# Issuing 32 small loads of decay rows from GpSimd instead of SyncE, in a fused attention and MLP kernel

## The chip, the cores and the metric

The kernel runs on one core of one Trainium2 chip. The metric is the device time of one launch in microseconds. The kernel before takes 765.26 us, the median of three runs (763.09 to 766.86). The execution that was profiled took 763.16 us, of which the span of its instructions is 761.2 us.

## The reference

Four sequences of 576 tokens go through causal attention with 8 heads of width 64 and a forget-gate decay, then through a first MLP with a layer norm and a residual, then through a gated MLP whose gate mixes the tokens.

```python
scores = scale * np.matmul(q, k.transpose(0, 1, 3, 2))
cum = np.cumsum(np.log(np.clip(f, 0.0001, 1.0)), axis=-1)
decay = cum[:, :, :, None] - cum[:, :, None, :]
scores = np.where(causal, -1000000000.0, scores + decay)
attn = np.exp(scores - max); attn = attn / (sum + 1e-09)
x = matmul(attn, v)                                   # 4 x 576 x 512
x = x + np.maximum(layernorm(x) * g_ln @ w_ch1, 0.0) @ w_ch2
h = np.maximum(x @ w_in, 0.0); u, v = halves of h
out = (u * (einsum('ts,bsd->btd', w_spatial, layernorm(v)) + b_spatial)) @ w_out
```

## The kernel before, in words

The 2304 tokens are cut into eight blocks of 256 tokens and a ninth part with the last 64 tokens of each sequence. For each block attention is computed, and its result goes through the first MLP in groups (`GROUPS`, seven groups of one block and one of two). The program emits attention of the blocks ahead and the MLP of a current group interleaved, by a table of positions (`SPAN`, `BEGIN`). A list scheduler then simulates the program and writes a fixed order of instructions for each engine: every engine, and every engine's queue of DMA issues, works its list strictly in order. The order is made when the kernel is built, so a change of one instruction's engine can move others.

Four blocks (the third kind, `attention`, lines 571 to 628) cover queries 256 to 575 of each sequence. They hold 4 x 8 = 32 heads, worked in 16 pairs, which this document numbers 0 to 15; pair k holds heads 2k and 2k+1. For each head `operands` (lines 325 to 343) loads q and k (line 330, tile `qk`), splits them into two operands for the scores, `x1` and `x2`, and loads four rows of cumulated decays into partitions 64 to 67 of `x2` (line 338). These rows make the decay part of the same matmul as the scores. Three buffers for `x2` are made once and filled with zeros (lines 332 to 335) and then taken in turn: `x2z0`, `x2z1`, `x2z2`, head h using buffer h modulo 3.

The scores are made in `weights` (line 359) as pairs of matmuls, one of `x2` and one of `x1`: for query tiles 2 and 3 head by head, and for tile 4 both heads of a pair together, in two column halves. So a pair has eight matmuls that read an x2 buffer, and the last of them frees the buffers of both heads. Head 2k takes the one freed by head 2k-3, and head 2k+1 the one freed by head 2k-2. With three buffers the end of pair k therefore starts two loads: that of head 2k+3, which is the second head of the next pair, and that of head 2k+4, the first head of the pair after it.

Behind the scores VectorE finds the row minimum (line 363), ScalarE takes the exponential (line 367), and the weights are written as two halves of 16 bits into `P16` (lines 319 and 380; five buffers). For tile 4 GpSimd first zeroes a part of `P16` (line 374). SyncE then transposes `P16` by DMA into `PT` (line 382), and the product with the values (line 586) follows later. The MLP's matmuls are at lines 864 and 849. At a group's end VectorE moves the sums out of PSUM (line 896, tile `t`), and GpSimd issues four DMAs that add them to the residual in DRAM (line 900). GpSimd also sums squares for the layer norm (lines 792 and 793). SyncE issues most loads of the stage: `qk`, the values `vr` (line 610), the decay rows, and the transposes.

Of the kernel before, what the change touches and what calls it, by code (L numbers as in the profile page):

```python
# [19 lines left out]
B, H, S, D = 4, 8, 576, 64  # L20
# [59 lines left out]
def f32(ap):  # L80
    return ap.bitcast(F32)
# [7 lines left out]
class Kernel:  # L89
# [235 lines left out]
    def operands(self, bh):  # L325

        nc, at = self.nc, self.at
        W, C = QW, QW + S
        qk = at.tile([P, C], F32, tag="qk", name="qk", bufs=BUFS["qk"])
        nc.sync.dma_start(out=qk, in_=self.qk[bh // H, bh % H])  # L330
        x1 = at.tile([P, C], F32R, tag="x1", name="x1", bufs=BUFS["x1"])
        if not self.x2z:
            for i in range(BUFS["x2"]):
                self.x2z.append(at.tile([P, C], F32R, name=f"x2z{i}"))
                nc.gpsimd.memset(f32(self.x2z[i][64:]), 0.0)
        x2 = self.x2z[0]
        self.x2z.append(self.x2z.pop(0))
        nc.sync.dma_start(out=f32(x2[64:68]), in_=self.decay_d[:, bh // (2 * H) * 2 * H + bh % H * 2 + bh // H % 2])
        self.copy(0, x1, qk)
        self.copy(0, x2[:64, :W], qk[:64, :W])  # L340
        nc.vector.tensor_tensor(out=x1[64:, :W], in0=qk[64:, :W], in1=f32(x1[64:, :W]), op=ALU.subtract)
        nc.vector.tensor_tensor(out=x2[:64, W:], in0=qk[:64, W:], in1=f32(x1[:64, W:]), op=ALU.subtract)
        return [(x[:, :W], x[:, W:]) for x in (x2, x1)]
# [1190 lines left out]
```

## Time and profile before

| | |
|---|---|
| median of three runs | 765.26 us (763.09 to 766.86) |
| profiled execution | 763.16 us, span 761.2 us |
| TensorE busy | 739.7 us (97%) |
| VectorE, ScalarE busy | 590.9 us (78%), 528.8 us (69%) |
| GpSimd busy | 67.4 us (9%), 102 instructions |
| decay rows | 32 issues on SyncE, 14 KB each, from 190.2 to 430.3 us |

The busy times are sums over the whole span. The stage of the 32 heads is the part from about 190 to 456 us. Times in the rows below count from the start of the span. A timeline merges like neighbours on an engine into one row, with their count behind the x; what stands in brackets is the idle time of the engine before the row and what ended it.

### The profile page before, as it was taken

The numbers are of one execution on the slowest core, as the hardware profiler recorded it, in microseconds if no ns is written. First come the engines' busy times: TensorE is split into PE (matmuls) and PEld (weight loads), VectorE is DVE, ScalarE is ACT, GpSimd is POOL, SyncE is SP. The second block draws the span as 40 slices with busy tenths as digits, with TensorE's granted clock in tenths as the row PEclk, the third lists the DMA queues.
The fourth block names the chain that finished last, engine by engine and source line by source line (L and its number), as shares of the span: only waits on it lengthen the run. The fifth ranks groups of instructions, "written<-read, shape, count | busy, mean of one in ns | idle before, by whom it ended". The sixth has DMA issues, their size and how long they took to land.

```text
span 761.2 us, 16265 instructions
## 1 busy us (share of the span) xinstructions
PE 739.7 (97%) x5912; PEld 567.9 (75%) x5912; DVE 590.9 (78%) x1569; ACT 528.8 (69%) x1320; POOL 67.4 (9%) x102
## 2 busy tenths in 40 slices
PE   8899998999999999999999999999999999999998
PEld 6788887888888877877888888644447678768686
DVE  7899799577599989989869845689456796785854
ACT  6898699576588989879857844587346764664633
POOL 6001100013102010110110100200012000000000
PEclk9999999999999999999999999999999999999999
DMA  8978694466589998988965944831025240100101
GB/s 263 295 269 274 206 266 84 89 171 105 176 167 206 198 220 183 195 189 177 201 144 116 148 84 149 213 132 56 1 22 111 70 125 1 44 21 7 57 2 62
DMA packets 164100, 104.68 MB, mean 138 GB/s; under 512 B 106147, under 2 KB 151299, under 8 KB 164021
## 3 DMA queue, kind: packets, MB, share of 16 engines
q1 hardware_dynamic: 153032, 93.06, 50.3%
q0 software_dynamic: 5376, 5.54, 5.2%
q10 hardware_dynamic: 5612, 5.06, 2.2%
q8 instruction: 46, 0.75, 0.4%
q14 instruction: 34, 0.27, 0.1%
HBM read 64.37 MB, written 15.11 MB: 104 GB/s over the span
## 4 chain that ended last, share of the span: by engine, by line
PE 63%; DVE 11%; ACT 10%; DMA 10%; issue 4%; SPq 2%; DVEq 0%; ACTq 0%
PE ph L864 16%; PE acc L849 12%; PE pb L808 8%; PE pb L809 8%; PE pb L810 8%; DMA raw<-in_moe_w_ch_dram 3%; PE s L359 3%; PE s L849 3%; DMA vr<-in_v_dram 2%; PE av L586 2%; ACT wt L744 2%; ACT P L319 2%; DMA x_d<-xT 2%; DVE P L380 1%; DMA qk<-decay 1%
## 5 line engine op out<-in xcount | busy, mean ns | idle before, releaser
L849 PE MATMUL acc<-hh,wt 128*128 128x256 f16 (+2 forms) x960 | 196.8, 295 | 3.2 <-ACT hh L875 3.2
L864 PE MATMUL ph<-xh,wt 128*128 128x256 f16 (+1 forms) x896 | 185.0, 288 | 2.0 <-DVE hl L879 2.0
L864 PEld LDWEIGHTS <-wt 128*128 128x128 f16 x1344 | 126.9, 98 | 47.4 <-issue 10.2
L849 PEld LDWEIGHTS <-wt 128*128 128x128 f16 x1344 | 128.7, 98 | 44.3 <-issue 5.3
L864 PE MATMUL ph<-xl,wt 128*128 128x256 f16 (+1 forms) x448 | 129.0, 288 | 0.0
L849 PE MATMUL acc<-hl,wt 128*128 128x256 f16 (+1 forms) x416 | 115.8, 281 | 1.1 <-DVE hl L879 1.1
L875 ACT ACTIVATE hh<-ph 128x256 f16<-128x256 f32 (+2 forms) x128 | 50.9, 397 | 45.8 <-PE ph L864 45.5
L879 DVE SCALAR_TENSOR_TENSOR hl<-ph,hh 128x256 f16<-128x256 f32 (+1 forms) x112 | 50.5, 453 | 35.9 <-ACT hh L875 35.7
L319 ACT ACTIVATE P<-sd,st 128x512 f16<-128x512 f32 (+2 forms) x128 | 70.6, 585 | 9.8 <-DVE st L370 6.9
L380 DVE SCALAR_TENSOR_TENSOR P<-sd,st,P 128x384 f16<-128x384 f32 (+2 forms) x96 | 59.2, 634 | 10.5 <-ACT P L319 10.3
L367 ACT ACTIVATE sd<-sd,st 128x384 f32<-128x384 f32 (+2 forms) x80 | 54.6, 682 | 14.4 <-DVE st L363 14.2
L359 PE MATMUL s<-x2z 128*128 128x384 f32 (+3 forms) x128 | 47.8, 382 | 1.9 <-DMA x2z<-decay_d 1.7
L363 DVE CUSTOM_DVE_ANT_0 sd<-s,mask 128x384 f32<-128x384 f32 (+2 forms) x80 | 46.0, 579 | 3.7 <-PE s L359 2.7
L900 POOL DMA_DIRECT2D x_d<-t x36 | 31.9, 1024 | 182.7 <-DVE t L896 153.1
L359 PE MATMUL s<-x 128*128 128x384 f32 (+3 forms) x128 | 41.4, 333 | 0.0
L809 PE MATMUL pb<-wsl,vh 128*128 128x288 f16 x128 | 36.6, 286 | 0.0
L808 PE MATMUL pb<-wsh,vl 128*128 128x288 f16 x128 | 36.6, 286 | 0.0
L810 PE MATMUL pb<-wsh,vh 128*128 128x288 f16 x128 | 36.4, 286 | 0.0
L810 PE MATMUL pb<-gh,woh 128*128 128x288 f16 x128 | 35.0, 286 | 0.0
L809 PE MATMUL pb<-gl,woh 128*128 128x288 f16 x128 | 35.0, 286 | 0.0
L808 PE MATMUL pb<-gh,wol 128*128 128x288 f16 x128 | 33.3, 286 | 0.0
L922 ACT ACTIVATE gh<-u 128x288 f16<-128x288 f32 x32 | 14.0, 437 | 26.5 <-DVE u L1261 26.5
(341 smaller groups left out, 1692.5 us busy)
## 6 DMA issues: line engine op xcount, KB each, us to landing
raw<-in_moe_w_ch_dram SPq DMA_DIRECT2D x32, 512.0 KB
qk<-in_qk_dram SPq DMA_DIRECT2D x32, 448.0 KB
vraw<-in_v_dram SPq DMA_DIRECT2D x5, 1024.0 KB
vr<-in_v_dram SPq DMA_DIRECT2D x16, 320.0 KB
x_d<-t POOLq DMA_DIRECT2D x36, 128.0 KB, 4.3
out_dram<-o SPq DMA_DIRECT2D x32, 144.0 KB
raw<-in_moe_w_in_dram SPq DMA_DIRECT2D x8, 512.0 KB
qk<-in_qk_dram SPq DMA_DIRECT2D x16, 192.0 KB
```

What stands on the lines that cost most here:

```text
L319: self.nc.scalar.activation(out, in_, AF.Copy, scale=scale)
L359: nc.tensor.matmul(ps[: R * u + R, : c1 - c0], lhsT=x[:, lo - q0 - R * u : hi - q0], rhs=y[:, c0:c1], start=g == 0, stop=g == len(heads[u] ...
L363: nc.vector.tensor_tensor_reduce(out=sd[:M, c0:c1], in0=ps[:M, : c1 - c0], in1=mask, scale=-0.125, scalar=3e38 if n == 0 else st[:M, n - 1 ...
L367: nc.scalar.activation(sd[:M, :N], sd[:M, :N], AF.Exp, bias=st[:M, n : n + 1], scale=-1.0, accum_out=st[:M, 2:3])
L380: low = nc.vector.scalar_tensor_tensor(out=dl, in0=src, scalar=rs, in1=dh, op0=ALU.mult, op1=ALU.subtract)
L808: first = mm(out, lhsT=al, rhs=bh, start=start, stop=False, **kw)
L809: mm(out, lhsT=ah, rhs=bl, start=False, stop=False, **kw)
L810: mm(out, lhsT=ah, rhs=bh, start=False, stop=stop, **kw)
L849: ins = nc.tensor.matmul(acc[m], lhsT=a, rhs=b, start=bank not in clear, stop=last and e == len(terms) - 1, skip_group_check=True)
L864: ins = nc.tensor.matmul(ph, lhsT=a, rhs=b, start=k == e == 0, stop=k == NK - 1 and e == len(terms) - 1)
L875: relu = nc.scalar.activation(hh, ph, AF.Relu)
L879: nc.vector.scalar_tensor_tensor(out=hl, in0=ph, scalar=0.0, in1=hh, op0=ALU.max, op1=ALU.subtract)
```

## The change

The DMA of the decay rows is issued by GpSimd and no longer by SyncE. The data, the tiles and the waits on the data are the same. Since the scheduler makes its lists anew, the lists differ from the first of these heads on: SyncE's has 32 entries fewer, GpSimd's 32 more, and those of the other engines hold the same instructions in a somewhat other order, up to the end of the stage.

```diff
         x2 = self.x2z[0]
         self.x2z.append(self.x2z.pop(0))
-        nc.sync.dma_start(out=f32(x2[64:68]), in_=self.decay_d[:, bh // (2 * H) * 2 * H + bh % H * 2 + bh // H % 2])
+        nc.gpsimd.dma_start(out=f32(x2[64:68]), in_=self.decay_d[:, bh // (2 * H) * 2 * H + bh % H * 2 + bh // H % 2])
         self.copy(0, x1, qk)
```

The first place is around the end of pair 9. GpSimd's list before, from the zeroing for pair 8 (`P16_4780`) over that for pair 9 (`P16_5058`) and pair 10 (`P16_5338`) to the sums of an MLP group:

```order
L374 MEMSET P16_4780 128x2x64
L792 TENSOR_TENSOR sq_4624<-sq_4624 128x512
L793 TENSOR_TENSOR sq_4624<-sq_4624 128x256
L374 MEMSET P16_5058 128x2x64
L374 MEMSET P16_5338 128x2x64
L900 DMA x2_d_70<-t_5465 128x256 x4
```

GpSimd's list after, at the same place. The two loads that pair 9 frees are the first of `x2z1` (head 22) and the first of `x2z0` (head 21); the other two are freed by pair 10:

```order
L374 MEMSET P16_4780 128x2x64
L792 TENSOR_TENSOR sq_4624<-sq_4624 128x512
L793 TENSOR_TENSOR sq_4624<-sq_4624 128x256
L374 MEMSET P16_5058 128x2x64
L338 DMA x2z1_2349<-decay_d_68 4x896
L338 DMA x2z0_2347<-decay_d_68 4x896 x2
L338 DMA x2z2_2351<-decay_d_68 4x896
L374 MEMSET P16_5338 128x2x64
L900 DMA x2_d_70<-t_5465 128x256 x4
```

The loads stand behind the zeroing for pair 9, and the load of head 21, which is needed first, stands behind that of head 22.

On SyncE's list before, the same two loads of the end of pair 9 stood behind the transposes of pairs 8 and 9 (`P16_4837`, `P16_4879` and `P16_4932` are the first three of pair 9):

```order
L382 DMA_TRANSPOSE PT_4557<-P16_4780 128x10x64
L382 DMA_TRANSPOSE PT_4667<-P16_4780 128x10x64
L382 DMA_TRANSPOSE PT_4819<-P16_4837 128x6x128
L382 DMA_TRANSPOSE PT_4819<-P16_4879 128x8x128
L382 DMA_TRANSPOSE PT_4912<-P16_4932 128x6x128
L338 DMA x2z0_2347<-decay_d_68 4x896
L338 DMA x2z1_2349<-decay_d_68 4x896
L330 DMA qk_5710<-in_qk_dram 128x896
```

After, SyncE goes from these transposes to the next one and then to the loads of `qk`:

```order
L382 DMA_TRANSPOSE PT_4557<-P16_4780 128x10x64
L382 DMA_TRANSPOSE PT_4667<-P16_4780 128x10x64
L382 DMA_TRANSPOSE PT_4819<-P16_4837 128x6x128
L382 DMA_TRANSPOSE PT_4819<-P16_4879 128x8x128
L382 DMA_TRANSPOSE PT_4912<-P16_4932 128x6x128
L382 DMA_TRANSPOSE PT_4912<-P16_4974 128x8x128
L330 DMA qk_5710<-in_qk_dram 128x896
```

Nothing else is moved between these transposes.

The second place is the end of pair 14. GpSimd's list before, with the zeroing for pairs 13 to 15 and the sums of two MLP groups:

```order
L374 MEMSET P16_6225 128x2x64
L374 MEMSET P16_6518 128x2x64
L900 DMA x2_d_70<-t_6421 128x256 x4
L374 MEMSET P16_6777 128x2x64
L900 DMA x2_d_70<-t_7183 128x256 x4
```

GpSimd's list after, from the two loads that pair 13 frees (heads 30 and 29):

```order
L338 DMA x2z0_2347<-decay_d_68 4x896
L338 DMA x2z2_2351<-decay_d_68 4x896
L374 MEMSET P16_6518 128x2x64
L900 DMA x2_d_70<-t_6421 128x256 x4
L338 DMA x2z1_2349<-decay_d_68 4x896
L374 MEMSET P16_6777 128x2x64
L900 DMA x2_d_70<-t_7183 128x256 x4
```

The load of `x2z1`, for head 31, the last one, stands behind all four sums of the MLP group.

## Rows read from the trace of the kernel before

**Rows 1.** Page, part 1: engine, busy us (share of the span), instructions.

```profile
PE 739.7 (97%) x5912; PEld 567.9 (75%) x5912; DVE 590.9 (78%) x1569; ACT 528.8 (69%) x1320; POOL 67.4 (9%) x102
```

**Rows 2.** Stretches: length, busy us of PE, PEld, DVE, ACT, POOL; clock, DMA, GB/s.

```profile
190.00:470.00 280.00, 273.49 (x2530) 227.26 (x2529) 224.81 (x611) 216.13 (x555) 26.04 (x40) 1.00 0.85 173
230.00:310.00 80.00, 77.17 (x719) 63.07 (x716) 74.59 (x205) 72.05 (x190) 10.46 (x15) 1.00 1.00 201
```

**Rows 3.** Waits of PE from 190 to 470: us, times, longest.

```profile
PE av L586 <- DMA PT<-P: 2.7, 2, 1.7
PE s L359 <- DMA x2z<-decay_d: 1.7, 2, 1.5
PE acc L849 <- DVE hl L879: 1.1, 1, 1.1
PE ph L864 <- DVE hl L879: 0.7, 1, 0.7
```

**Rows 4.** Waits of SyncE's queue at line 338: us, times, longest.

```profile
SPq L338 <- PE s L359: 3.6, 2, 3.1
```

**Rows 5.** Timeline of SyncE's queue around two loads: start, us, what.

```profile
339.59 6.58 SPq L382 DMA_TRANSPOSE PT<-P  x5
346.27 0.76 SPq L338 DMA_DIRECT2D x2z<-decay_d  x2
...
430.33 0.70 SPq L338 DMA_DIRECT2D x2z<-decay_d  x1
```

**Rows 6.** Chain that ended last, 336 to 380: start, us, what.

```profile
346.27 2.01 DMA x2z<-decay_d
...
351.23 1.68 PE av L586 x30
...
353.67 1.31 PE ph L864 x12
...
356.29 1.06 PE s L359 x8
...
373.04 5.58 DMA x2z<-decay_d
```

**Rows 7.** Timeline of PE at the ends of pairs 9, 11 and 14.

```profile
339.43 0.29 PE L359 MATMUL s<-x2z 128*64 128x288 f32 x1
...
348.41 0.41 PE L359 MATMUL s<-x2z 128*128 128x384 f32 x1 [1.49 <-DMA x2z<-decay_d]
...
378.76 0.41 PE L359 MATMUL s<-x2z 128*128 128x384 f32 x1 [0.26 <-DMA x2z<-decay_d]
...
426.44 0.27 PE L849 MATMUL acc<-hh,wt 128*128 128x256 f16 x1
...
435.22 0.41 PE L359 MATMUL s<-x2z 128*128 128x384 f32 x1
```

**Rows 8.** Timeline of GpSimd, at the ends of pairs 9 and 14.

```profile
344.21 0.20 POOL L374 MEMSET P<- 128x128 f16 x1 [3.96 <-DMA PT<-P]
...
428.38 2.66 POOL L900 DMA_DIRECT2D x_d<-t  x3 [2.27 <-DVE t L896]
...
433.43 0.85 POOL L900 DMA_DIRECT2D x_d<-t  x1 [2.38 <-DVE ls L632]
```

**Rows 9.** Line 900: issue ns min/median/max; landing overall, 300:310, 425:435.

```profile
L900 POOL DMA_DIRECT2D x_d<-t x36: 847/882/1730, 112.3 to 574.0; - x36
...
DMA to landing us min/median/max: 3.1/4.3/7.0
...
DMA to landing us min/median/max: 3.5/5.3/5.9
...
DMA to landing us min/median/max: 4.7/5.4/7.0
```

**Rows 10.** Timeline of VectorE: the last two of a group's four sums.

```profile
428.81 0.87 DVE L896 TENSOR_SCALAR t<-acc,und 128x256 f32<-128x256 f32 x2
```

**Rows 11.** VectorE's instruction on the x2 buffers: ns min/median/max.

```profile
L342 DVE TENSOR_TENSOR x2z<-qk,x x32: 744/751/752, 200.5 to 431.6; 64x576 fp32r<-64x576 f32 x32
```

## The prediction, made before the changed kernel ran

> **What bounds the kernel.** The busy times come first: TensorE works 97% of the span [rows 1]. The stretches then tell where the rest is: in the stage with the 32 heads, 190 to 470 us, TensorE is busy 273.5 of 280 us [rows 2], so it idles 6.5 us there, and the clock is granted in full. The change touches nothing outside this stage, so no removal of waits can win more than 6.5 us. In its densest part, 230 to 310 us, VectorE and ScalarE are busy 93% and 90%, and the DMA engines 100% [rows 2]: little is free there to catch up. Next come the waits of TensorE [rows 3]: those that name a releaser sum to 6.2 us, and 1.7 of them, in two pieces, are for the decay rows. The first piece is 1.49 us, at the second head of pair 10; the second is 0.26 us in pair 12 [rows 7]. The chain shows what they were: a load of 2.01 us that was issued late, and one of 5.58 us that landed late [rows 6]. SyncE's timeline says why the first was late: pair 9 freed the buffers at 339.7 us (339.43 plus 0.29, [rows 7]), but the queue was in five transposes until 346.2 [rows 5].
>
> So TensorE sets the end, and this change counts by what it waits for: the time from the last scores of a pair, which free two buffers, to the first scores of the next pair's second head, which need one of the two loads.
>
> **What the loads cost on SyncE, and what goes.** The 32 issues leave SyncE's queue, with 3.6 us of waits for scores [rows 4]. SyncE is not the bound; what it can give TensorE is an earlier transpose, and TensorE waits 2.7 us in all for those [rows 3]. I take 0.7 us of gain, between 0 and 2.7: two waits only, and their transposes wait mostly for their inputs. The 1.75 us for the decay rows are taken out in full, and what the new loads make TensorE wait is added anew.
>
> **What a load costs on GpSimd.** No load of decay rows was issued there. The nearest rows are the MLP's sums, 128 KB each: 0.88 us of issue, and 3.1 to 7.0 us from issue to landing; in two of the busy groups 3.5/5.3/5.9 and 4.7/5.4/7.0 [rows 9]. A load moves 14 KB, no sums, so it should be near the short end: I take 3.5 us. The bounds are 2.0, the same load on SyncE [rows 6], and 5.4 us. The two loads of a pair's end stand in GpSimd's list with the one needed later in front, since its buffer comes free one matmul sooner. The needed one lands 0.3 us (the last matmul) + 0.9 (the other's issue) + 3.5 = 4.7 us after the pair's last scores begin.
>
> How much time there is, the new order of TensorE tells with the old durations: 12 matmuls of the MLP take 1.31 us, 8 of the scores 1.06, 30 of the values 1.68 [rows 6], so some 0.11 to 0.13 us a matmul of MLP or scores. From the last scores of pair k to those that need the load, the new order has 65, 39, 47, 50, 70, 48, 55, 50, 81, 49, 54, 110, 80, 108 and 72 matmuls (k = 0 to 14): 7.7, 4.9, 5.7, 6.1, 6.5, 6.0, 6.6, 6.0, 7.8, 6.1, 6.5, 11.0, 9.6, 10.7 and 6.8 us. All exceed 4.7. GpSimd's own list holds up three of them:
>
> - After pair 2 one of the MLP's sums stands between the two loads: 1.2 us more (one of the longer issues, within the 1.73 of [rows 9]). 5.9 against 5.7: a wait of 0.2 us; with 5.4 for the landing, 2.1.
> - After pair 9 the loads stand behind the zeroing of pair 9's buffer, which waits for the transposes of pair 8; it began at 344.21 [rows 8], 4.8 us after the pair's last scores at 339.43 [rows 7]. Then 0.2 + 0.9 + 3.5 give 9.4 us, against 6.1: a wait of 3.3. The new order of VectorE writes pair 8's weights before those of the next tile instead of behind, and some 1.3 us sooner against TensorE's list; I take 2.0 us of wait, between 0 and 3.9.
> - After pair 14 the load of the last head stands behind all four sums of an MLP group. The fourth does not start with its data: VectorE had written the last of `t` by 429.7 [rows 10], yet the issue began at 433.43, just after the first of the four, issued at 428.38, could have landed (4.7 us, the shortest of this group) [rows 8, 9]. This pattern stands in all five groups of this stretch: the fourth begins 0.2 to 0.4 us after the first has landed, as if GpSimd's queue held three such DMAs. The group's last matmul began at 426.44, so the fourth issue starts 7.0 us later, the load 0.9 after it, and lands at 7.9 + 3.5 = 11.4. In the new order 91 matmuls, 9.0 us, lie from there to the scores that need it (86 and 8.8 us before, 426.44 to 435.22 [rows 7]). A wait of 2.4 us, between 0.5 (landing in 2.0 us, and 0.4 off) and 4.3. Before, SyncE issued this load at 430.33 [rows 5], free of the sums, and TensorE did not wait.
>
> GpSimd's issues themselves, 32 x 0.88 = 28 us, lie in an engine that is busy 26 of 280 us [rows 2]; what is queued behind a waiting load is a zeroing, and behind it one transpose of SyncE. The zeroing for a pair stood within some 5 us behind the pair's last scores before, and its loads are freed at those scores, so I cost it at nothing.
>
> **The reordering.** TensorE's list keeps its pace: the last scores of every pair from 8 on stand within 1 us of where they stood, counted in matmuls. I take it as 0, within 3 us either way.
>
> **The sum.** -1.75 - 0.7 + 0.2 + 2.0 + 2.4 = +2.2 us against the profiled 763.16 us (761.2 of span and 2.0 around it), that is 765.3. The median of the runs lies 2.1 us above that execution, so I predict 767.4 us for a median.
>
> **A rule that speaks against the change.** VectorE's instruction on these buffers takes 744 to 752 ns in all 32 cases [rows 11], and GpSimd's issues 847 to 1730 ns beside a VectorE busy 93% [rows 9, 2]: the worst is 0.85 us over the median. The Trainium skill, "SBUF — State Buffer", section "SBUF: two separate sides", says that GpSimd cannot write its descriptors while VectorE holds the port they share, and gives a DMA that grew from 620 to 3100 ns. The largest issue here agrees in direction and not in size.
>
> **Rivals.**
>
> 1. *Slower: the loads land late.* If a load lands in 5.4 us, as the sums of the busy groups do, the needed one comes at 6.6 us and misses the scores after nine of the pairs: 1.7 (pair 1), 2.1 (2), 0.5, 0.1, 0.6, 0.6, 0.1 (3, 4, 5, 7, 10), 3.9 (9) and 4.3 (14), 13.9 us, less 2.45: +11.5, 776.8 us. For it: the DMA engines are full there [rows 2]. Against it: the size of the load. It decides from a landing of 4 us on, where the sum passes 3.8 us.
> 2. *Slower: VectorE holds up the issues.* If each issue takes the longest 1.73 us, the needed load comes 1.7 us later: about 1.5, 1.9, 0.3, 0.4, 0.4, 3.7 and 3.3 us of waits, 11.5 less 2.45: +9, 774.3 us. The page "SBUF — State Buffer" of the Trainium skill, section "SBUF: two separate sides", has the rule that would make it so.
> 3. *Faster: the own queue pays.* The load that took 5.58 us on SyncE lay between transposes and loads of `qk`; on a queue of its own it may take 2.0, and the transposes move up. Then 1.75 and nearly all of the 2.7 us go, and 0.5 to 1 comes back at pair 14: -3.6, 761.7 us. Against it: the lists above.
> 4. *Nothing that can be measured:* the loads arrive in time everywhere, and only the 1.75 us change places: 765 us.
>
> **How the numbers follow.** A measurement of this kernel can tell 0.5%, 3.8 us, from no change. The forecast has 0.40: three quarters of it, 0.30, lies within 3.8 us, and 0.10 above, since its waits reach 3.9 and 4.3 at their upper bounds. Rival 4 has 0.17, all within. Rival 3 has 0.15, of which 0.12 beyond 3.8. Rival 1 has 0.20 and rival 2 has 0.08, both slower. That gives faster 0.12, same 0.50, slower 0.38. The range runs from rival 3's time, 761.5, to just above rival 1's, 778.0, with about a tenth left out at either side; the forecast's own range is 764 to 772.
>
> **What would show it.** Right: GpSimd's line 338 with 32 issues near 0.9 us and landings of 3 to 4 us; TensorE waiting for decay rows at pair 15 (about 2.4 us) and pair 10 (about 2), and hardly elsewhere; the fourth sum of a group again 3 to 5 us behind the first. Wrong: no wait at pair 15, or one at most pairs, or TensorE's idle time moved to other releasers than the decay rows, which would be the reordering that I took as nothing.

## The result: 0.6% slower, and the profile after

The changed kernel took 769.67 us, the median of 8 runs (767.85 to 772.59), and the kernel before 763.6 us on the same chip; the ratio is 1.0062, 95% interval 1.004 to 1.0083. The forecast was 767.4 us, in a range of 761.5 to 778. The slowdown was foreseen at 2.2 us and is 4.7 by the ratio (the two medians lie 6.1 apart), just above the 0.5% that tell a change from none. The forecast of 767.4 us started from a median of 765.26 in three runs; with five more that median is 763.6, so the two times look closer than the two changes are. The profiled execution took 768.64 us (span 766.9), 5.5 more than that of before. Ratios below are to the kernel before, run beside each version, with the 95% interval in brackets.

First the page's part 1 and the stretches of after, with the columns of [rows 1, 2].

```profile
PE 741.2 (97%) x5912; PEld 570.7 (74%) x5912; DVE 593.5 (77%) x1569; ACT 529.9 (69%) x1320; POOL 83.6 (11%) x134
```

```profile
190.00:470.00 280.00, 269.97 (x2504) 225.64 (x2502) 226.36 (x609) 214.59 (x552) 40.93 (x69) 1.00 0.86 170
230.00:310.00 80.00, 75.09 (x683) 61.23 (x682) 72.97 (x201) 70.89 (x183) 16.55 (x28) 1.00 1.03 194
```

TensorE works nearly as much as before. In the stage of the heads it idles 10.0 us where it idled 6.5 [rows 2], at full clock in this execution. These 3.5 us are the larger part of the 5.7 by which the span grew; 1.5 are busy time, and 0.7 idle time outside the stage. The waits in the stage, as in [rows 3]:

```profile
PE s L359 <- DMA x2z<-decay_d: 3.0, 2, 2.1
PE ph L864 <- DVE hl L879: 2.2, 3, 1.0
PE av L586 <- DMA PT<-P: 1.9, 3, 1.0
PE av L586 <- ACT P L319: 1.3, 1, 1.3
PE s L359 <- DVE x2z L342: 0.6, 1, 0.6
PE ph L864 <- DVE xl L828: 0.4, 1, 0.4
PE s L359 <- DVE st L363: 0.3, 1, 0.3
PE acc L849 <- ACT hh L875: 0.3, 1, 0.3
```

The waits for decay rows are 3.0 us where they were 1.7, and those for everything else 7.0 where they were 4.5 [rows 3]. So the larger part of the added waits does not stand at the loads at all. Line 338 itself, now on GpSimd, with its issue (ns) and its landings (us):

```profile
L338 POOL DMA_DIRECT2D x2z<-decay_d x32: 497/519/1520, 186.8 to 435.3; - x32
...
DMA to landing us min/median/max: 2.1/3.3/6.5
```

GpSimd's timeline at the ends of pairs 2, 9 and 14 shows what stands ahead of a load, as in [rows 8]:

```profile
241.21 1.82 POOL L900 DMA_DIRECT2D x_d<-t  x2 [9.64 <-DVE t L896]
242.38 1.18 POOL L338 DMA_DIRECT2D x2z<-decay_d  x1
242.91 1.55 POOL L900 DMA_DIRECT2D x_d<-t  x1
243.47 1.52 POOL L338 DMA_DIRECT2D x2z<-decay_d  x1
...
346.63 0.20 POOL L374 MEMSET P<- 128x128 f16 x1 [2.64 <-DVE st L363]
347.15 0.51 POOL L338 DMA_DIRECT2D x2z<-decay_d  x1 [0.32 <-PE av L757]
...
430.22 2.73 POOL L900 DMA_DIRECT2D x_d<-t  x3 [1.76 <-DVE t L896]
434.75 0.84 POOL L900 DMA_DIRECT2D x_d<-t  x1 [1.80 <-DVE x2z L342]
435.29 0.83 POOL L338 DMA_DIRECT2D x2z<-decay_d  x1
```

And TensorE where it needs these loads, as in [rows 7]: at pair 3 it waits, at pair 10 not, at pair 15 a little.

```profile
249.76 0.41 PE L359 MATMUL s<-x2z 128*128 128x384 f32 x1 [2.12 <-DMA x2z<-decay_d]
...
351.46 0.42 PE L359 MATMUL s<-x2z 128*128 128x384 f32 x1
...
439.56 0.41 PE L359 MATMUL s<-x2z 128*128 128x384 f32 x1 [0.93 <-DMA x2z<-decay_d]
```

The chain of waits between 240 and 252 us has the load of pair 3 on it, 6.16 us from issue to landing, where 3.5 were expected:

```profile
243.47 6.16 DMA x2z<-decay_d
```

### The profile page after: what moved, and what is told of

Read it like the earlier page. It is cut to its first block, busy times and chain, and to the rows that moved or that the text cites. A ratio compares the mean times of both kernels' runs of the same rounds, so it can differ in the third digit from the quotient of the medians.

```text
span 766.9 us, 16266 instructions
## 1 busy us (share of the span) xinstructions
PE 741.2 (97%) x5912; PEld 570.7 (74%) x5912; DVE 593.5 (77%) x1569; ACT 529.9 (69%) x1320; POOL 83.6 (11%) x134
## 3 DMA queue, kind: packets, MB, share of 16 engines
q1 hardware_dynamic: 152776, 92.60, 50.8%
## 4 chain that ended last, share of the span: by engine, by line
PE 67%; DVE 10%; DMA 9%; ACT 8%; issue 4%; POOL 1%; SPq 1%; DVEq 0%; ACTq 0%; POOLq 0%
PE ph L864 15%; PE acc L849 14%; PE pb L808 8%; PE pb L810 8%; PE pb L809 8%; DMA PT<-P 3%; PE s L359 2%; PE av L586 2%; PE s L532 2%; DVE x2z L342 2%; PE s L849 1%; DMA x2z<-decay_d 1%; DVE P L380 1%; DMA raw<-in_moe_w_in_dram 1%; DVE sd L363 1%
## 5 line engine op out<-in xcount | busy, mean ns | idle before, releaser
L319 ACT ACTIVATE P<-sd,st 128x512 f16<-128x512 f32 (+1 forms) x128 | 70.5, 586 | 9.8 <-DVE st L370 6.1
L380 DVE SCALAR_TENSOR_TENSOR P<-sd,st,P 128x384 f16<-128x384 f32 (+1 forms) x96 | 58.5, 631 | 7.5 <-ACT P L319 7.4
L586 PE MATMUL av<-PT,vp 128*64 128x320 f16 (+2 forms) x480 | 29.3, 269 | 3.2 <-DMA PT<-P 1.9
```

The lines of the kernel that those rows point to most:

```text
L319: self.nc.scalar.activation(out, in_, AF.Copy, scale=scale)
L380: low = nc.vector.scalar_tensor_tensor(out=dl, in0=src, scalar=rs, in1=dh, op0=ALU.mult, op1=ALU.subtract)
```

## The experiments

Two theories. **A**: the loads land late in GpSimd's queue, behind the MLP's sums, and these waits are the loss. **B**: the scheduler, which orders all engines anew once the loads have moved, chose an order that costs more. The change alters the engine of 32 instructions, but with it what stands at 1653 of the 5604 positions of TensorE's list. (The expected texts put the two waits of the changed kernel at 2.3 and 1.1 us; the timeline above has 2.12 and 0.93.) To part the two, the next kernels fix each engine's order by a list:

```diff
+    def keep_order(self):        # called at the end of run()
...
+            for d in steps:      # steps: an engine's order, read from a list
...
+                    self.tc.add_manual_dep(ins, prev.name, dep, reason="order")
```

**The new order, loads on SyncE.** The load's line is that of the kernel before; the list is that of the changed kernel. The 32 loads stand in no list, so the scheduler places them on SyncE.

> The loads of decay rows stay on SyncE, while TensorE, ScalarE, VectorE, GpSimd and the rest of SyncE issue in exactly the order that the changed kernel has. It isolates the order. Theory A (the loads come late in GpSimd's queue, the order costs nothing): as before, 762 to 765 us, ratio to the kernel before 1.000 +-0.002, and PE's waits for decay rows are small, at most the 2.3 us of before, with none at pair 3. Theory B (the new order that the scheduler chose costs the time): 766.5 to 769 us, ratio 1.004 to 1.007, and the first score again 2.4 us later than in the kernel before. If both have a share, about 766, ratio 1.003.

Ratio 1.0046 (1.0017 to 1.0076), median 768.07 us. B has a share. It is no clean price of the order, though: with the loads on SyncE the new order has late loads of its own, at pairs 4 and 8, issued behind five and six transposes. The first scores come 9.7 us after the last matmul of the stage ahead (line 555) and not 7.4, as theory B said; the new order has 21 more matmuls before them.

```profile
PE s L359 <- DMA x2z<-decay_d: 3.7, 2, 2.0
```

**The old order, loads on GpSimd.** The load's line is that of the changed kernel, GpSimd's list too; the other engines have the list of the kernel before.

> The loads are issued by GpSimd, whose order is that of the changed kernel, while TensorE, ScalarE, VectorE and the rest of SyncE issue in exactly the order of the kernel before. It isolates the queue. Theory A (late loads): 767 to 769 us, ratio to the kernel before 1.004 to 1.007, with PE's waits for decay rows of 2 us or more at pair 3 and about 1 us at pair 15. Theory B (order): the waits at pairs 3 and 15 are there (3.2 us), but the 1.7 us of waits at pairs 10 and 12 and about 0.7 us of waits for transposes are gone, so 763.5 to 765 us, ratio 1.000 to 1.002.

Ratio 1.0094 (1.0066 to 1.0121), median 770.03 us: the queue costs without any reordering, so A has a share too. The waits are not where either theory put them: none at pair 3, but 2.5 at pair 12 and 2.7 at pair 15, both behind sums; the load for pair 12 landed 7.2 us after its issue. How much work TensorE's order puts in between decides whether a late load is waited for: counted as in the prediction, the old order has 74 matmuls before the scores of pair 3 that need the load and 54 before those of pair 12, the new order 47 and 110. In the changed kernel a load for pair 12 landed after 6.5 us, and TensorE did not wait.

```profile
PE s L359 <- DMA x2z<-decay_d: 5.1, 2, 2.7
```

**The old order, loads on GpSimd ahead of the sums.** As the last, with three loads moved in GpSimd's list (x_d is one of the four sums, load(h) the load of head h; the ends of pairs 2 and 14):

```diff
-x_d x_d load(8) x_d load(7) x_d  ...  x_d x_d x_d x_d load(31)
+load(8) load(7) x_d x_d x_d x_d  ...  load(31) x_d x_d x_d x_d
```

> As the kernel with GpSimd's loads in the old order, but in GpSimd's list the two loads at the end of pair 2 and the one at the end of pair 14 stand ahead of the four MLP sums there. If the sums ahead of the loads are what makes them late, the waits at pairs 3 and 15 go (3.2 us): 760 to 762.5 us under theory B, ratio to the kernel before 0.996 to 0.999, and 764 to 766 under theory A where late loads cost more than their waits. If a load lands late for another reason (its issue by GpSimd alone), the waits at pairs 3 and 15 stay above 1 us and the time equals that of the kernel with GpSimd's loads in the old order.

Ratio 1.0041 (1.0019 to 1.0064), median 766.82 us. It beats the kernel with the sums ahead, and its waits for decay rows are down to 0.4 us, 1.3 below those of the kernel before; yet it is slower than that kernel. Its profile is of an execution of 773.12 us, the longest of eleven, and has 3.8 us of waits for transposes and 2.2 for ScalarE, so it says little of the typical one.

**Room for four sums in GpSimd's queue.** The changed kernel with one number altered:

```diff
-dynamic_dma_scratch_size=1024
+dynamic_dma_scratch_size=1216
```

> The changed kernel, all orders the same, with 1216 in place of 1024 bytes for GpSimd's DMA descriptors. If the fourth MLP sum waits because the descriptors of three fill that space, the fourth is now issued about 0.6 us behind the third (434.75 becomes about 432), the load of head 31 about 3 us earlier, and the wait of 1.1 us at pair 15 goes, at pair 3 part of the 2.3 us: 766 to 768.5 us where the changed kernel has 769.7. If the fourth waits for something else, issue times and time stay as in the changed kernel.

Ratio 1.0079 (1.0059 to 1.0099), median 769.8 us. The space was what the fourth sum waited for: here all four are issued in a row (GpSimd's timeline at the end of pair 14), the fourth 0.5 us behind the third and not 3.4.

```profile
432.80 3.57 POOL L900 DMA_DIRECT2D x_d<-t  x4 [1.67 <-DVE t L896]
435.13 1.78 POOL L338 DMA_DIRECT2D x2z<-decay_d  x1
```

But the load behind them landed 7.4 us after its issue, not 4.1, so the wait at pair 15 stayed (1.3 us). At pair 3 TensorE waited 1.8 us, which the profile puts down to ScalarE (line 367); the load, landed 5.6 us after its issue, came only 0.1 us ahead of the scores. The wait for room had only been a wait outside the queue: the load at pair 15 landed 0.4 us behind the fourth sum, so what takes the time is the sums being carried out ahead of it.

```profile
DMA to landing us min/median/max: 7.4/7.4/7.4
```

**No loads, in either order.** The decay rows are loaded for the first three heads alone and left out for the other 29, so both orders can be compared with hardly a load on any queue.

```diff
-        nc.sync.dma_start(out=f32(x2[64:68]), in_=...)
+        if bh < 3:
+            load = nc.sync.dma_start(out=f32(x2[64:68]), in_=...)
```

> Decay rows are loaded for the first three heads alone, so the 29 other loads are left out (the later heads work with old rows); all engines keep the order of the kernel before. It prices the loads as they stood on SyncE. If their price is the wait that PE shows for them (1.7 us) and what SyncE gains for its transposes: 760.5 to 762.5 us, ratio to the kernel before 0.996 to 0.999. If other waits step in where the loads go, as they seem to do where GpSimd's loads came early and the time was still above that of before: 763 to 765 us, ratio 0.999 to 1.002.

> The same with 29 loads left out, and all engines in the order of the changed kernel. It prices the order with no load in it on either queue. Theory B (the order itself costs): 2 to 4 us above the old order without loads, ratio to the kernel before 1.001 to 1.004. Theory A (the order costs nothing; with the loads on SyncE in the new order it was the loads' own delay behind transposes, 3.7 us of waits, that cost): within 1 us of the old order without loads. The difference between the changed kernel (ratio 1.006) and this one is then the price of the 29 loads on GpSimd: 2 to 3 us by the waits of 3.0 us at pairs 3 and 15.

Old order: 0.9971 (0.9954 to 0.9988), median 762.5 us. New order: 1.0005 (0.9989 to 1.0021), median 764.43. This is the cleanest pair of the study: the new order by itself costs 0.34%, 2.6 us (some 0.8 to 4.4 by the two intervals; the medians lie 1.9 apart), the loads on SyncE cost 0.29%, 2.2 us, where they were, and those on GpSimd 0.57%, 4.4 us, in the new order (1.0062 less 1.0005). With the kernels above, as ratios to the kernel before:

| loads | old order | new order |
|---|---|---|
| none but the first three | 0.9971 | 1.0005 |
| SyncE | 1 | 1.0046 |
| GpSimd, as in the changed kernel | 1.0094 | 1.0062 |
| GpSimd, ahead of the sums | 1.0041 | 1.0062 |

The rows do not add up to one price for the order and one for the queue. The new order costs 0.34% with few loads and 0.46% with them on SyncE, but with the loads on GpSimd as in the changed kernel it takes 0.32% less than the old one (intervals that overlap): it was made for that placement.

**The changed kernel with the loads ahead of the sums** (the same move in GpSimd's list as above).

> The changed kernel, all orders the same but for GpSimd's: the two loads at the end of pair 2 and the one at the end of pair 14 stand ahead of the four MLP sums there. If the sums ahead in the queue make those loads late: no wait for decay rows above 0.5 us at pairs 3 and 15, and 2 to 3 us less than the changed kernel: 766 to 768 us, ratio to the kernel before 1.002 to 1.004. If other waits of PE take their place: 769 to 770, ratio 1.006, with the waits for transposes and for VectorE grown by what the others lost.

Ratio 1.0062 (1.0041 to 1.0083), median 768.2 us: nothing gained. GpSimd's timeline shows the move, and the landings after pair 2 and after pair 14 show that it worked:

```profile
241.79 0.99 POOL L338 DMA_DIRECT2D x2z<-decay_d  x2 [10.53 <-PE s L359]
242.77 2.71 POOL L900 DMA_DIRECT2D x_d<-t  x3
...
434.02 0.51 POOL L338 DMA_DIRECT2D x2z<-decay_d  x1 [3.70 <-PE s L359]
434.52 2.75 POOL L900 DMA_DIRECT2D x_d<-t  x3
```

```profile
DMA to landing us min/median/max: 3.1/3.1/3.2
...
DMA to landing us min/median/max: 2.1/2.1/2.1
```

The loads that landed after 6.2 and 4.1 us now land after 3.1 and 2.1, and both waits are gone. Others have come in their place (waits of TensorE, 190 to 470 us; the 0.6 us for a load are at pair 4, where it landed 5.6 us after its issue, behind the fourth of the sums that now follow):

```profile
PE av L586 <- DMA PT<-P: 3.3, 4, 1.1
PE ph L864 <- DVE hl L879: 2.3, 3, 1.0
PE av L586 <- ACT x L319: 2.2, 1, 2.2
PE s L359 <- DMA x2z<-decay_d: 0.6, 1, 0.6
```

The longest of them stands at the values of pair 3 (TensorE's timeline):

```profile
270.74 0.30 PE L586 MATMUL av<-PT,vp 128*64 128x320 f16 x1 [2.16 <-ACT x L319]
...
272.12 3.25 PE L586 MATMUL av<-PT,vp 128*64 128x320 f16 x29 [0.87 <-DMA PT<-P]
```

This hole does not need the loads. The kernel with few loads in the new order has it at the same place, 73.0 us after the last matmul of the stage ahead (line 557 here; 74.0 in the kernel above), and the one in the old order has a smaller one there, after 71.4 us:

```profile
271.77 0.30 PE L588 MATMUL av<-PT,vp 128*64 128x320 f16 x1 [2.15 <-ACT x2z L319]
```

```profile
268.67 0.30 PE L588 MATMUL av<-PT,vp 128*64 128x320 f16 x1 [1.20 <-ACT x2z L319]
```

Nor is it the new order's alone. The kernel before waits 1.68 us at these values, for a transpose (at 268.40, the 1.7 of [rows 3]), and the old order with loads on GpSimd ahead of the sums 2.24. In the changed kernel the same values began after 73.1 us with a wait of 0.3, because TensorE had already lost its 2.1 us at pair 3. So the wait for the load and the wait at the values look like one hole that shows at whichever comes first. A second price shows in the stretches around it, of the kernel with the loads ahead of the sums (busy us of PE, PEld, DVE, ACT, POOL; then the clock):

```profile
268.00:270.00 2.00, 0.57 (x6) 0.27 (x3) 1.79 (x5) 2.00 (x5) 0.00 (x0) 1.00 0.97 158
270.00:272.00 2.00, 0.51 (x2) 0.20 (x2) 1.96 (x6) 1.23 (x4) 0.00 (x0) 0.96 1.06 149
272.00:274.00 2.00, 1.88 (x16) 1.25 (x18) 0.93 (x3) 0.00 (x0) 0.20 (x1) 0.50 1.21 298
274.00:276.00 2.00, 2.00 (x20) 1.80 (x17) 0.08 (x1) 0.59 (x3) 0.00 (x0) 0.68 1.01 360
```

After 4 us in which TensorE was busy about a quarter of the time, the granted clock fell from 2.4 to 1.2 GHz (0.50), and 29 matmuls of the values took 3.25 us, where 30 take 1.68 [rows 6]. The kernel with few loads in the new order falls in the same way behind its 2.15 us, and once more behind three waits of 0.38, 0.25 and 1.04 us, which the changed kernel has too, there without a fall (the last row):

```profile
272.00:274.00 2.00, 1.88 (x16) 1.57 (x17) 1.96 (x6) 0.81 (x3) 0.20 (x1) 0.63 0.69 138
274.00:276.00 2.00, 2.00 (x21) 1.88 (x18) 0.34 (x2) 0.46 (x2) 0.00 (x0) 0.52 1.20 281
...
310.00:314.00 4.00, 4.00 (x25) 2.71 (x25) 3.49 (x12) 3.44 (x10) 0.00 (x0) 0.57 1.18 215
```

Each of the two falls costs some 1.7 us of full clock (2 us at 0.63 and 2 at 0.52; 4 at 0.57). The old order with few loads has no wait above 1.2 us in the stage, and no stretch of 4 us between 258 and 350 us below full clock. In these two profiles the waits of TensorE from 190 to 470 us that name a releaser sum to the same 5.7 us; what sets the new order apart there is the two falls. But the new order's profile is of an execution of 767.28 us, the longest of twelve.

**Two loads on GpSimd, the rest as before.** The two loads that made TensorE wait longest in the kernel before; the order is its own.

```diff
-        nc.sync.dma_start(out=f32(x2[64:68]), in_=...)
+        (nc.gpsimd if bh in (21, 22) else nc.sync).dma_start(out=f32(x2[64:68]), in_=...)
```

> The kernel before in its own order, but the two loads at the end of pair 9 (heads 21 and 22), the ones behind which PE waited longest in it (1.5 us at pair 10), are issued by GpSimd, ahead of its zeroing memset; the other 30 stay on SyncE. Landing within 3.3 us of an issue at about 341, the wait at pair 10 goes: 1.5 us less than the kernel before, 761.5 to 763 us, ratio 0.997 to 0.999. If what follows at pair 10 (a transpose or VectorE) is as late, the ratio is 1.000 +-0.001.

Ratio 1.0012 (0.9991 to 1.0033), median 764.37 us: no gain. GpSimd's timeline and TensorE's show that the wait at pair 10 (1.49 us, [rows 7]) is gone:

```profile
344.23 1.09 POOL L338 DMA_DIRECT2D x2z<-decay_d  x2 [0.61 <-PE s L359]
```

```profile
350.62 0.42 PE L359 MATMUL s<-x2z 128*128 128x384 f32 x1
```

In its profile 0.96 us came back at pair 12, where 0.26 had been waited, and 2.37 at the values of pair 3, where it had been 1.68. Neither this nor any other version that loads all rows beat the kernel before.

## Why the prediction came out as it did

**Right.** The direction, slower, and that TensorE would wait for decay rows at a few places that GpSimd's list sets, and no longer at pair 12. The matmuls counted between the pairs are those of the trace. The issue costs less than assumed (0.52 us in the median, not 0.88), and the median landing is 3.3 us for 3.5 taken. Rival 2 fell with that: the longest of the 32 issues took 1520 ns, and it stood among sums. The Trainium skill, "SBUF — State Buffer", section "SBUF: two separate sides", has VectorE keep GpSimd from writing descriptors and gives a DMA of 3100 ns in place of 620; the trace shows no such delay in most issues, with a median of 519 ns, a shortest of 497 and a VectorE busy 91% from 230 to 310 us. Rival 1, late landings at nine pairs, came true in part: landings above 4.5 us, four of the 32, came only behind sums, and TensorE waited at two pairs; rivals 3 and 4 fell with the time, though the first half of rival 4, loads in time nearly everywhere, was right.

**Pair 15: the mechanism was right, the size was not.** 2.4 us were predicted and 0.93 came. The load landed 9.2 us after the first sum's issue (435.29 and 4.1, less 430.22), nearly as in the working (9.5); but TensorE had 8.4 us of work from there to the scores (439.56 less 0.93, less 430.22), where the working had 7.1 (9.0 from 426.44, so less 1.9). That GpSimd's queue holds three such DMAs was inferred from a pattern and is shown by the kernel with more room.

**Pair 3: the step that failed among the waits.** 0.2 us were predicted, 2.12 came. The working counted the sum between the two loads as 1.2 us of issue and let the load land as fast as one that is alone. The time that TensorE had was as worked out, 5.8 us for 5.7 (the last scores of pair 2 began at 241.88). But a load with sums ahead of it in the queue lands after them: 6.16 us here, 4.1 at pair 15, 7.4 with four sums issued in a row ahead, each time 0.2 to 1.2 us behind the last of these sums, and 3.1 and 2.1 for the same loads with no sum ahead. The Trainium skill, "DMA: Bandwidth & Descriptors", section "SWDGE vs HWDGE vs iDMA", says that only one queue is allocated to GpSimd's DMAs; the trace agrees, with loads and sums in one queue (5376 packets before the change and 6400 after it). A price of issue is not the price of standing behind.

**Pair 10: predicted 2.0 us, measured none.** The zeroing ahead of the loads began 1.1 us after pair 9's last scores (345.50) and not 4.8: TensorE came to these scores 6.1 us later than before, the zeroing only 2.4 (346.63 for 344.21). It was close: the needed load landed at some 351.2 us, and its scores began at 351.46.

**The reordering: taken as 0, measured at 2.6 us.** This is the largest miss, though within the 3 us allowed. The step asked only whether the scores keep their place among TensorE's matmuls, and they do. It did not ask where the new order makes TensorE wait for the other engines, nor what the clock does behind such a wait: with few loads in it, the hole at the values of pair 3 is 2.15 us for 1.20, and in that profile two falls of the clock set the new order apart. How much of the price they are in the mean is open. Over 12 runs each, the mean granted clock was 0.9984 in the old order with few loads and 0.9964 in the new. That is an estimated 1.4 us at the rate given at the end, but only 0.4 at the rate within these two kernels' own runs (0.2 us for each 0.001). Where the rest stands was not settled.

**The credit of 1.75 us.** It was taken out in full because TensorE waited it. The loads cost 2.2 us in all where they were, so the size is right for all of them together; but taking away the largest wait alone (1.49 us) won nothing that can be measured, nor did taking away 2.4 us of waits in the changed kernel. This suggests, and no run shows it alone, that a wait is worth no more than the time until the next thing that TensorE needs is late as well.

**The sum.** Order +2.6, loads on GpSimd +4.4, loads on SyncE -2.2: +4.8, where the prediction had +2.2. That this meets the 4.7 is no test, since the three are differences of the same ratios. Going through the table the other way, the queue costs 7.2 us in the old order, and the new order gives 2.4 back. So both theories have a share, but how much each has cannot be said by itself. Why the loads on GpSimd cost 4.4 us in the new order even ahead of the sums is open: there the waits for transposes are 3.3 us, with few loads 0.7. That the measured time lies within the forecast's own range (764 to 772) is partly luck: the three new waits were put at 4.6 us and came to 3.0, which hid part of the order's price.

## What to carry to other kernels

Price a DMA moved to another queue by what stands ahead of it there until that has landed, not by its own issue. Where a scheduler orders the engines, a change of one instruction's engine is also a new order: fix the order by a list to compare the two, in both orders, since the prices need not add up, and leave the work out altogether to see what it costs. And where three engines and the DMAs are each busy nine tenths, a wait removed may be worth only the distance to the next wait: look for that one before crediting it.

## What was not expected of the hardware

- GpSimd issues a load of 4 rows of 3584 bytes in 0.50 us when alone, less than a sum of 128 KB (0.85); beside sums the same load took up to 1.52 us, and 1.78 behind four in a row.
- The same 32 loads were 32 packets each on GpSimd's queue (5376 to 6400 in all) and 8 each on SyncE's (153032 to 152776).
- A transpose occupies SyncE's queue for 1.2 to 2.9 us, whatever else is queued: 1.21 and 2.93 also occur in the kernel with no decay loads.
- The mean granted clock of a run lay between 0.991 and 1.0 in all kernels; over 22 runs of the kernel before, the time rises by 0.7 us for each 0.001 less. The kernel with the loads ahead of the sums had 0.9943 in the mean of its six runs, the changed kernel 0.9975: an estimated 2.2 us at this rate, nearly the 2.4 us of waits that it removed. Its own six runs do not show the rate (0.2 us), so this is not settled. In the changed kernel's own profile the wait of 2.12 us at pair 3 did not bring the clock down (1.00 from 230 to 310 us); what decides that was not tried.
